# Storing zeros ahead of the result, and last weights in pieces of 5, 2 and 1 eighths, in a decode kernel bound by loads

## The chip, the cores and the metric

The kernel runs on one core of one Trainium2 chip. The metric is the device time of one execution in microseconds (us), as a median of several runs. "The span" is the time from the first to the last instruction in one profiled execution; it is about 1.3 us shorter than the device time. All times inside a profile count from the start of its span.

## The reference, cut to what matters

```python
def reference(A_x, A_k_cache, A_v_cache, A_wq, A_wo, B_x, B_w_in, B_w_sp, B_b_sp, B_w_out, gate_w):
    # A: one token, 32 query heads, 4 key/value heads, 65536 cached positions of 128
    # B: a gated MLP (gelu, layernorm, gate) from 1024 to 3584 and back to 1024
    x = A_x
    g = _sigmoid((x * gate_w).sum(-1, keepdims=True))
    a = _A_ref(x, A_k_cache, A_v_cache, A_wq, A_wo)   # ... attention, then @ wo (4096 x 1024)
    b = _B_ref(x, B_w_in, B_w_sp, B_b_sp, B_w_out)
    return g * a + (1 - g) * b                        # 1 x 1 x 1024, bf16: 2 KB
```

162 MB of caches and weights are read, and 2 KB are written. Nothing but the reading can take long.

## The kernel before: the parts that matter here

The kernel is written with a small recorder. `P(engine, instruction, r=..., w=...)` records one operation with the names that it reads and writes, and semaphore waits are made from these names. All large loads go through the sync queue (SP) in one fixed order, into a ring of SBUF. The last to come are the output weights `wo`, in four parts of 2 MB. The fourth part is cut into pieces, so that PE has little left to do when the last bytes land:

```python
    for i in range(3):
        load([("wo", i, 0)], rows(A_wo, i, 8), VB + 8 * DO * i)
    s3 = kring()
    for c0, c1 in [(0, 4), (4, 6), (6, 8)]:
        load([("wo", 3, c0)], rows(A_wo, 3, 8)[:, DO * c0:DO * c1], s3 + DO * c0)
    # ... everything else of the kernel ...
    for i, c0, c1 in [(0, 0, 8), (1, 0, 8), (2, 0, 8), (3, 0, 4), (3, 4, 6), (3, 6, 8)]:
        sl, keys = use(("wo", i, c0))

        def f(e, i=i, sl=sl, c0=c0, c1=c1):
            for c in range(c0, c1):
                for q in range(4):                    # four column groups of PE, side by side
                    o = DO * (c - c0) + QW * q
                    ins = e.matmul(fb[32 * q:32 * q + 1, 0:QW], ovec[:, 8 * i + c:8 * i + c + 1],
                                   sl[:, o:o + QW], start=False, stop=(i == 3 and c == 7),
                                   tile_position=(0, 32 * q), skip_group_check=True)
            return ins
        P("PE", f, r=[("ovec", i)] + keys, w=["fb"])
        done(("wo", i, c0))
    P("DVE", lambda e: e.tensor_copy(orow[0:97, :], fb[0:97, 0:QW]), w=["orow", "fb"])
    osrc = bass.AP(tensor=arena, offset=OFF["OROW"], ap=[[32 * NA, 4], [1, QW]])
    P("SP", lambda e: e.dma_start(out[0, 0].rearrange("(q n) -> q n", n=QW), osrc), r=["orow"], w=["out"], dma="out")
```

One eighth of a part is 1024 columns: 256 KB, and 4 matmuls on PE. The result lies in 4 rows (partitions 0, 32, 64 and 96) of 256 values, so the store moves 4 rows of 512 bytes.

The waits are emitted in the order of the names, reads first, then writes.

```python
                for d in ws:                          # ... in Recorder.emit
                    if d.dma:
                        handle.wait_ge(dsem[d.dma[0]], d.dma[1])
                    else:
                        handle.wait_ge(sems[d.eng], d.count)
                last = o.fn(handle)
```

## Time and profile before

The median was 383.87 us in 3 runs. These are the lines of the page of the kernel before that say what bounds it: the span in 40 slices (DMA: busy tenths of the 16 DMA engines; GB/s: what they moved), the DMA totals, and the queues with packets, MB and share of the 16 engines' time.

```profile
DMA  9999999999999999999999999999999999999995
GB/s 384 439 435 425 423 417 435 439 436 433 439 425 418 432 430 439 439 432 432 429 420 429 435 439 434 429 435 426 422 432 437 435 432 429 439 425 420 423 425 220
DMA packets 6246, 162.16 MB, mean 424 GB/s; under 512 B 728, under 2 KB 732, under 8 KB 988
...
q1 hardware_dynamic: 6200, 162.01, 98.8%
q8 instruction: 8, 0.13, 0.1%
q14 instruction: 2, 0.02, 0.0%
```

The DMA engines are busy in every slice but the last. The loads set the pace of everything except what follows the last bytes.

The tail is the only place where this change can act. These are the last lines of the chain of waits of the kernel before (start, length, what).

```profile
351.47 28.03 DMA arena<-in_A_wo_dram
379.50 0.04 issue
379.54 0.63 PE fbt L706 x8
380.17 0.02 issue
380.19 0.42 DVE arena L712
```

And this is the line of its timeline for the store behind the cast.

```profile
380.64 0.63 SPq L714 DMA_DIRECT2D out_dram<-arena  x1
```

The last load was issued at 351.47, stood in the queue behind some 25 us of other loads, and landed at 379.50. From there on every step is in series: 8 matmuls, cast, issue of the store, the store's flight. The span ends at 382.33, so the tail behind the landing is 2.83 us.

### The profile page before, as it was taken

What the parts mean: (1) busy time and instruction counts of PE and PEld (TensorE: products, weight loads), DVE (VectorE), ACT (ScalarE), POOL (GpSimd) and SP (SyncE); (2) the same over time, 40 slices, a digit from 0 to 9 for tenths busy, and PEclk for the clock granted to TensorE, in tenths of its full rate; (3) what the DMA queues carried; (4) which work ended last, traced back from release to release, by engine and by line L of the source; (5) the groups of instructions that cost most, each with busy time, mean ns of one, the idle gap of its engine ahead of it and who ended that gap; (6) DMA issues with size and microseconds to landing.
All of it is one profiled execution on the core that took longest, in us unless ns stands there. A gap on an engine that the chain in (4) does not pass through costs nothing.

```text
span 382.3 us, 2522 instructions
## 1 busy us (share of the span) xinstructions
PE 234.6 (61%) x1375; PEld 56.9 (15%) x785; DVE 211.7 (55%) x229; ACT 25.3 (7%) x39; POOL 1.5 (0%) x8
## 2 busy tenths in 40 slices
PE   0055754286687578545793777377938673849344
PEld 0011111111121111101120112012201121112121
DVE  6116952785781698067935980579448914842020
ACT  1000000102030001000210010001200100031000
POOL 1000000000000000000000000000000000000000
PEclk9996998689979599959898998786979988778695
DMA  9999999999999999999999999999999999999995
GB/s 384 439 435 425 423 417 435 439 436 433 439 425 418 432 430 439 439 432 432 429 420 429 435 439 434 429 435 426 422 432 437 435 432 429 439 425 420 423 425 220
DMA packets 6246, 162.16 MB, mean 424 GB/s; under 512 B 728, under 2 KB 732, under 8 KB 988
## 3 DMA queue, kind: packets, MB, share of 16 engines
q1 hardware_dynamic: 6200, 162.01, 98.8%
q8 instruction: 8, 0.13, 0.1%
q14 instruction: 2, 0.02, 0.0%
q10 hardware_dynamic: 36, 0.00, 0.0%
HBM read 162.01 MB, written 0.00 MB: 424 GB/s over the span
## 4 chain that ended last, share of the span: by engine, by line
DMA 61%; PE 19%; DVE 18%; SPq 1%; ACT 1%; issue 1%
DMA arena<-in_A_k_cache_dram 33%; DVE arena L476 13%; DMA arena<-in_B_w_in_dram 8%; DMA arena<-in_A_wo_dram 7%; DMA arena<-in_B_w_out_dram 6%; PE obt L246 6%; DMA arena<-in_A_wq_dram 6%; PE obt L248 5%; PE scp L246 4%; PE scp L248 4%; DVE arena L493 1%; SPq L365 1%; DVE arena L514 1%; DVE arena L464 1%; DVE arena L549 0%
## 5 line engine op out<-in xcount | busy, mean ns | idle before, releaser
L476 DVE STREAM_TRANSPOSE arena<-arena 128x2048 f32<-128x2048 f32 x64 | 145.5, 2295 | 84.5 <-DMA arena<-in_A_k_cache_dram 71.9
L246 PE MATMUL scp<-arena 128*128 128x512 bf16 x256 | 112.5, 439 | 83.4 <-DVE arena L476 61.0
L248 PE MATMUL scp<-arena 128*128 128x512 bf16 x256 | 111.0, 434 | 0.0
L246 PE MATMUL obt<-arena 128*64 128x512 bf16 (+2 forms) x334 | 64.6, 428 | 30.6 <-DMA arena<-in_A_v_cache_dram 12.4
L248 PE MATMUL obt<-arena 128*64 128x512 bf16 (+2 forms) x334 | 64.1, 424 | 0.0
L246 PEld LDWEIGHTS scp<-arena 128*128 128x128 bf16 x256 | 27.5, 107 | 192.2 <-DVE arena L476 93.8
L509 ACT ACTIVATE arena<-arena 128x1024 bf16<-128x1024 f32 x16 | 18.4, 1148 | 237.5 <-DVE arena L505 127.4
L246 PEld LDWEIGHTS obt<-arena 128*64 128x64 bf16 (+1 forms) x334 | 19.4, 116 | 86.6 <-issue 79.1
L493 DVE TENSOR_SCALAR_CACHE_REDUCE arena<-scp 128x1024 f32<-128x1024 f32 x16 | 19.3, 1205 | 9.3 <-PE scp L248 9.3
L514 DVE STREAM_TRANSPOSE arena<-arena 128x1024 bf16<-128x1024 bf16 x16 | 19.4, 1214 | 9.0 <-PE obt L248 6.4
L706 PE MATMUL fbt<-arena 128*1 128x256 bf16 x128 | 6.2, 339 | 5.9 <-DMA arena<-in_A_wo_dram 5.7
L539 DVE RECIPROCAL arena<-mbt 128x1 f32<-128x1 f32 x4 | 0.6, 139 | 14.0 <-PE mbt L535 14.0
L441 DVE CAST arena<-obt 97x1024 bf16<-97x1024 f32 x1 | 1.2, 1224 | 11.5 <-PE obt L248 11.5
L712 DVE CAST arena<-fbt 97x256 bf16<-97x256 f32 x1 | 0.4, 425 | 11.3 <-PE fbt L706 11.3
L588 DVE COPY arena<-obt 128x896 f32<-128x896 f32 x1 | 1.1, 1093 | 9.1 <-PE obt L248 9.1
L464 DVE COPY arena<-arena 32x32 bf16<-32x32 bf16 x16 | 2.7, 166 | 6.2 <-PE scp L248 6.0
L407 PE MATMUL scp<-arena 8*128 8x1 bf16 x8 | 0.6, 197 | 8.4 <-DVE arena L402 8.4
L706 PEld LDWEIGHTS fbt<-arena 128*1 128x1 bf16 x128 | 2.8, 93 | 8.8 <-DMA arena<-in_A_wo_dram 6.7
L595 ACT ACTIVATE arena<-arena 128x28 f32<-128x28 f32 x1 | 0.2, 226 | 52.4 <-DVE arena L594 52.4
L549 DVE SCALAR_TENSOR_TENSOR arena<-obt,arena 128x512 bf16<-128x512 f32 x4 | 3.0, 751 | 0.1
L601 PE MATMUL mbt<-arena 128*128 128x1 f32 x2 | 0.4, 260 | 4.3 <-DVE arena L600 4.3
L509 ACT ACTIVATION_READ_ACCUMULATOR arena<-arena 128x1 f32 x16 | 3.0, 186 | 0.0
(88 smaller groups left out, 47.0 us busy)
## 6 DMA issues: line engine op xcount, KB each, us to landing
arena<-in_A_k_cache_dram SPq DMA_DIRECT2D x16, 4096.0 KB, 38.4
arena<-in_A_v_cache_dram SPq DMA_DIRECT2D x16, 4096.0 KB, 31.1
arena<-in_A_wq_dram SPq DMA_DIRECT2D x2, 4096.0 KB, 16.8
arena<-in_A_wo_dram SPq DMA_DIRECT2D x3, 2048.0 KB, 22.6
arena<-in_B_w_in_dram SPq DMA_DIRECT2D x1, 4096.0 KB, 25.2
arena<-in_B_w_out_dram SPq DMA_DIRECT2D x1, 3584.0 KB, 23.1
arena<-in_B_w_in_dram SPq DMA_DIRECT2D x1, 3072.0 KB, 32.2
arena<-in_A_wo_dram SPq DMA_DIRECT2D x1, 1024.0 KB, 26.5
```

The costliest lines, as they stand in the source:

```text
L246: return e.matmul(*a, **kw)
L248: one = e.matmul(*a, **kw).ins
L365: P("SP", lambda e, o=OFF["RING"] + off + c, m=m, src=src[:, c:c + m]: e.dma_start(arena[:, o:o + m], src), w=[("slot", x) for x in grains ...
L441: P("DVE", lambda e: e.tensor_copy(psb[0:97, :], ob[0:97, :]), w=["psb", "ob"])
L464: P("DVE", lambda e, pb=pb: e.tensor_copy(vw(qpad, 24 + 32 * pb, [[QP, 4], [1, 8]], 32 * pb, 32), vw(qall, 8 * g, [[32, 4], [1, 8]], 32 * ...
L476: P("DVE", lambda e: e.transpose(ktb(i).bitcast(F32), sl[:, 4096 * p:4096 * (p + 1)].bitcast(F32)), r=keys[2 * p:2 * p + 2], w=[("kt", i % ...
L493: P("DVE", lambda e: e.tensor_scalar(scs(n), sc_ps(n), 0.0, None, op0=ALU.add, op1=ALU.max, accum_out=maxc[:, n:n + 1]), w=[("sc", n % NSC ...
L509: P("ACT", lambda e: e.activation(psb, scs(n), ACTF.Exp, bias=gcol(n // NP, K_NB), scale=SCALE, accum_out=lp[:, n:n + 1]), r=[("sc", n % N ...
L514: P("DVE", lambda e: e.transpose(ptsb(n), psb), r=["psb"], w=[("ptsb", n % 2)])
L549: P("DVE", lambda e: e.scalar_tensor_tensor(osc, ob[:, 512:1024], gcol(g, K_FB), osc, op0=ALU.mult, op1=ALU.add), r=[("fh", g, 1), "psb"], ...
L588: P("DVE", lambda e: e.tensor_copy(vw(zr, 0, [[FB4, 2], [32, FC], [1, 32]]), vw(ob, 0, [[512, 2], [1, FC], [FC, 32]])), w=[KZR, "ob"])
L706: ins = e.matmul(fb[32 * q:32 * q + 1, 0:QW], ovec[:, 8 * i + c:8 * i + c + 1], sl[:, o:o + QW], start=False, stop=(i == 3 and c == 7), ti ...
```

## The change

The intent is to shorten that tail in two places. The fourth part of `wo` is cut 5+2+1 instead of 4+2+2, so that only 4 matmuls remain behind the last landing. And the output is stored twice: once with zeros while the last weights are still loading, and once with the result, so that the second store finds whatever is slow at first use already paid for. The smaller bookkeeping grain (`GRAN`) is needed because 5 eighths is no multiple of 2048 columns.

```diff
+    P("POOL", lambda e: e.memset(orow, 0.0), w=["orow"])
...
-    GRAN = 2048
+    GRAN = 1024
...
-    for c0, c1 in [(0, 4), (4, 6), (6, 8)]:
+    for c0, c1 in [(0, 5), (5, 7), (7, 8)]:
         load([("wo", 3, c0)], rows(A_wo, 3, 8)[:, DO * c0:DO * c1], s3 + DO * c0)
+
+    osrc = bass.AP(tensor=arena, offset=OFF["OROW"], ap=[[32 * NA, 4], [1, QW]])
+
+    def store():
+        P("SP", lambda e: e.dma_start(out[0, 0].rearrange("(q n) -> q n", n=QW), osrc), r=["orow"],
+          w=["out"], dma="out")
...
+            if n == len(stream) - 1:
+                store()
...
-          r=keys[2 * p:2 * p + 2], w=[("kt", i % NKT)])
+          r=keys[4 * p:4 * p + 4], w=[("kt", i % NKT)])
...
-    for i, c0, c1 in [..., (3, 0, 4), (3, 4, 6), (3, 6, 8)]:
+    for i, c0, c1 in [..., (3, 0, 5), (3, 5, 7), (3, 7, 8)]:
...
-    osrc = bass.AP(tensor=arena, offset=OFF["OROW"], ap=[[32 * NA, 4], [1, QW]])
-    P("SP", lambda e: e.dma_start(out[0, 0].rearrange("(q n) -> q n", n=QW), osrc), r=["orow"], w=["out"], dma="out")
+    store()
```

## The prediction

> **What bounds the kernel.** The 16 DMA engines: on the page they are busy 9 tenths or more in 39 of 40 slices, at a mean of 424 GB/s for 162 MB. The change touches none of these bytes, so only the tail behind the last weights can move. From the timeline and the trace's single instructions and packets (us from the span's start):
> - The last weights' last packet ends at 379.05, their semaphore lands at 379.50, the first of the last 8 matmuls starts at 379.54.
> - These 8 (256 columns) end at 380.14: two rounds of four column groups, 0.21 us from round to round, at a granted clock of 0.5. The skill's page "TensorE: Matmul & The Clock Gate" gives N / 1.2 GHz for a cold array, 0.213 us: trace and page agree.
> - The cast takes 0.42 us, to 380.62.
> - The output store's issue takes 0.63 us (380.64 to 381.28). Its first packet follows 0.60 us later; the skill's page "DMA: Bandwidth & Descriptors" (latency table) says about 600 ns to the first byte, and the trace agrees. Its last semaphore count comes at 382.29; the span ends at 382.33.
>
> **Pieces of 5, 2, 1 eighths for 4, 2, 2.** The last piece has 4 matmuls, one round, for 8. Its landing should stay near 379.5 (packets of 2 KB for 4 KB: estimate +0.02 us). The first piece lands one eighth later (about 377.64), its 20 matmuls take about 1.24 us, to 378.9; the middle piece lands about there and its 8 matmuls end near 379.5, just when the last piece lands. PE is not late and one round is saved: -0.21 us, all on the critical path.
>
> **The store of zeros.** The sync queue's 43 load issues mostly take 0.33 us (after a wait) or 0.43 (back to back), also where a tensor is read for the first time; the store alone takes 0.63. On the ACT queue the first issue took 0.58 us, the next three 0.27 to 0.29, though they too use few engines. So I take about 0.3 of the 0.63 us for a first use (of this kind of DMA on this queue), which the store of zeros pays at about 351.5, where 25 us of loads are queued and nobody waits. The final issue should fall to 0.33 to 0.43: -0.25 us (estimate). I expect no gain in the 0.60 us to the first packet or the 0.33 us from packet to semaphore.
>
> **Costs.** Four 512-byte packets and their semaphore writes between the last two loads: at most +0.04 us (26 and 9 ns each in the final store). The cast now also waits for the first store's landing, which should come before 379.3, ahead of the cast's start at 379.98. The memset on idle POOL and the finer bookkeeping cost nothing.
>
> **Sum.** -0.21 -0.25 +0.06 = -0.4: last instruction near 381.9. Time 383.45 us, range 382.95 to 383.95 (the runs before spread over 0.4). Faster by over 2%: 0.01; within 2%: 0.98; slower: 0.01.
>
> **What shows each step.** PE's last group has 4 matmuls, about 0.38 us long, starting at the last landing. The final store's issue takes 0.33 to 0.43 us, the first's about 0.6. The cast waits for PE, not for the first store. DMA stays at 424 GB/s.
>
> **What would make it wrong.** The 0.63 us may belong to the kind of store (to DRAM, on four engines), not to a first use: then only -0.15. The zeros may land late behind loads and hold the cast. The first packet of a second write may come earlier: up to -0.3 more. The DMA engines end 1.3 us apart; a drift there may hide it all.

## The result

The changed kernel took 383.59 us (median of 5 runs, 383.43 to 383.75) against 383.75 us before (383.64 to 384.15). The ratio is 0.9993, with a 95% interval of 0.9981 to 1.0005. The interval is 0.9 us wide. The time alone cannot tell whether anything was won; the tails in the traces can, because they repeat to a few thousandths of a us (two traces of each kernel, below). Each tail is read from one profiled execution.

These are the last lines of the chain of waits of the changed kernel.

```profile
350.67 0.62 SPq L349
351.29 0.05 issue
351.34 28.46 DMA arena<-in_A_wo_dram
379.80 0.04 issue
379.84 0.41 PE fbt L715 x4
380.25 0.03 issue
380.28 0.02 DVEq L109
380.30 0.04 issue
380.35 0.42 DVE arena L721
```

And these are the lines of its timeline of the sync queue for the store of zeros, the last load, and the store of the result.

```profile
350.67 0.62 SPq L349 DMA_DIRECT2D out_dram<-arena  x1
351.34 0.39 SPq L374 DMA_DIRECT2D arena<-in_A_wo_dram  x1
380.80 0.54 SPq L349 DMA_DIRECT2D out_dram<-arena  x1
```

Read against the lines of before, four things have moved:

- The last load lands at 379.80, 0.30 us later. This was not forecast.
- PE's last group has 4 matmuls and takes 0.41 us instead of 0.63: -0.22 us.
- Between PE and the cast a line "DVEq L109" has appeared: a wait that stands in an instruction of its own. The cast starts 0.12 us after the last matmul instead of 0.05.
- The final issue takes 0.54 us instead of 0.63.

The profiled span even grew, from 382.33 to 382.42 us. So the questions are: what delayed the landing, what did each half of the change do, and what did the store of zeros warm.

### The profile page after: what moved, and what is told of

Its sections match the earlier page's. It is cut to its first block, busy times and chain, and to the rows that moved or that the text cites. A ratio compares the mean times of both kernels' runs of the same rounds, so it can differ in the third digit from the quotient of the medians.

```text
span 382.4 us, 2525 instructions
## 1 busy us (share of the span) xinstructions
PE 229.7 (60%) x1375; PEld 56.3 (15%) x785; DVE 211.2 (55%) x229; ACT 25.3 (7%) x39; POOL 1.8 (0%) x9
## 4 chain that ended last, share of the span: by engine, by line
DMA 61%; DVE 21%; PE 16%; SPq 1%; issue 1%; ACT 1%; DVEq 0%
DMA arena<-in_A_k_cache_dram 34%; DVE arena L485 15%; DMA arena<-in_B_w_in_dram 8%; DMA arena<-in_A_wo_dram 7%; PE obt L246 6%; DMA arena<-in_B_w_out_dram 6%; PE obt L248 6%; DMA arena<-in_A_wq_dram 6%; PE scp L246 2%; PE scp L248 2%; DVE arena L502 1%; DVE arena L523 1%; SPq L374 1%; DVE arena L558 1%; DVE arena L473 1%
## 5 line engine op out<-in xcount | busy, mean ns | idle before, releaser
L246 PE MATMUL scp<-arena 128*128 128x512 bf16 x256 | 108.7, 425 | 90.7 <-DVE arena L485 65.7
L248 PE MATMUL scp<-arena 128*128 128x512 bf16 x256 | 107.3, 419 | 0.0
L563 PE MATMUL mbt<-arena 128*128 128x128 bf16 x16 | 1.8, 239 | 2.3 <-DVE arena L558 2.3
```

The source lines that it names most:

```text
L246: return e.matmul(*a, **kw)
L248: one = e.matmul(*a, **kw).ins
L563: ins = e.matmul(mb[:, 0:128], sel[:, 128 * c:128 * (c + 1)], osc[:, 128 * c:128 * (c + 1)], start=(c == 0), stop=(c == 3))
```

## The experiments

Eleven kernels ran. The first table gives what the trace shows of each tail; every number is a difference of two times in that trace. "Landing" is the last semaphore count of the last load, "tail" the time from there to the end of the span. "To cast" runs from the end of the last matmul to the start of the cast. "To packet" runs from the end of the final store's issue to its first data packet. "Final issue" is the time that the queue's instruction takes; it is not a separate step ahead of the packet, as "The other queue" shows, so the two columns are best added.

| kernel | landing | tail | last matmuls | to cast | final issue | to packet |
|---|---|---|---|---|---|---|
| before | 379.50 | 2.828 | 0.596 | 0.054 | 0.633 | 0.598 |
| before, again | 379.53 | 2.824 | 0.597 | 0.049 | 0.633 | 0.595 |
| after | 379.80 | 2.622 | 0.383 | 0.120 | 0.535 | 0.636 |
| after, again | 379.59 | 2.619 | 0.383 | 0.121 | 0.536 | 0.639 |
| pieces only | 379.52 | 2.611 | 0.383 | 0.054 | 0.628 | 0.597 |
| zeros only | 379.68 | 2.841 | 0.595 | 0.123 | 0.536 | 0.640 |
| after, waits swapped | 379.47 | 2.552 | 0.383 | 0.051 | 0.535 | 0.639 |
| zeros in two halves | 379.83 | 2.637 | 0.383 | 0.152 | 0.514 | 0.641 |
| pieces, store on ACT | 379.75 | 2.615 | 0.383 | 0.052 | 0.582 | 0.645 |
| pieces, DVE padded | 380.56 | 2.596 | 0.383 | 0.053 | 0.615 | 0.596 |
| pieces, small loads | 379.59 | 2.582 | 0.383 | 0.049 | 0.557 | 0.645 |
| pieces, cast and store on ACT | 379.68 | 2.564 | 0.382 | 0.053 | 0.580 | 0.644 |
| after, cast and stores on ACT | 379.56 | 2.508 | 0.382 | 0.054 | 0.521 | 0.644 |

### Both kernels once more

The edit is none: both kernels ran again unchanged, to learn what repeats.

> The unchanged kernel once more, for a second trace and for the noise of the comparison. Theory (the moment at which the last weights land moves from run to run by a few tenths of a us, because instruction fetches of 16 and 8 KB hold up single DMA engines): the 16 landings of the last load again fall in two groups, 7 early and 9 late by 1.3 to 1.9 us, with one outlier; the last landing lies anywhere from 379.4 to 379.9 us; the store's issue is 0.63 us again. Rival (the landing moved by +0.30 us because of the change): the last landing is 379.50 within 0.05 us. Time ratio 1.000 within 0.001 under both.

Measured: 383.74 us (5 runs) against 383.86 (9 runs of before), ratio 0.9999 (0.9985 to 1.0013). The tail was 2.824 us, the issue 0.633 us, and the landing 379.53. A landing this close to 379.50 fits the rival as well as the theory, so this run does not decide between them; the next one does.

> The changed kernel once more. Theory of varying landings: the last landing is not bound to 379.80, it may fall to 379.5; the rest of the tail repeats: 0.38 us of matmuls, 0.12 us from the last matmul to the cast, 0.53 us for the final store's issue. Rival (change delays the landing): 379.80 within 0.05 us again. Time ratio 0.9990 to 1.0000.

Measured: 383.56 us, ratio 0.9994 (0.9981 to 1.0006). The tail was 2.619 us against 2.622, but the landing moved from 379.80 to 379.59.

What follows: the tail repeats from run to run of a kernel, and the landing does not. The change shortens the tail by 0.206 us (2.828 to 2.622, and 2.824 to 2.619 in the second pair).

### Each half of the change alone

The pieces alone:

```diff
     # the changed kernel, less:
-    P("POOL", lambda e: e.memset(orow, 0.0), w=["orow"])
-            if n == len(stream) - 1:
-                store()
```

> The pieces of 5, 2 and 1 eighths alone, no store of zeros. Both theories: last group of 4 matmuls, 0.38 us; the cast starts 0.05 us after the last matmul (no second wait); the only store's issue takes 0.62 to 0.64 us. From the tail behind the landing this is -0.21 us against before, so ratio 0.9994 within 0.0006 if the landing does not move. If 2 KB packets delay the landing, it lies 0.1 us or more past that of before.

Measured: 383.53 us against 383.86, ratio 0.9993 (0.9980 to 1.0005). The tail is 2.611 us, and the landing, at 379.52, is not delayed by the 2 KB packets. The end of the chain of waits, and the store in the timeline of the sync queue:

```profile
379.56 0.41 PE fbt L712 x4
379.98 0.02 issue
380.00 0.42 DVE arena L718
...
380.45 0.63 SPq L348 DMA_DIRECT2D out_dram<-arena  x1
```

The zeros alone:

```diff
-    for c0, c1 in [(0, 5), (5, 7), (7, 8)]:
+    for c0, c1 in [(0, 4), (4, 6), (6, 8)]:
     # ... and the same pieces in the loop of the matmuls
```

> The store of zeros alone, with pieces of 4, 2 and 2 eighths. Theory: last group of 8 matmuls, 0.60 us; cast 0.12 us after the last matmul, +0.07 for the second wait; final issue 0.53 us, -0.10; sum about -0.03 us, ratio 1.0000 within 0.0006. Rival (zeros delay the landing): the last landing lies at 379.7 or later, and the engine that ends last is one of those that carry a packet of the zeros; ratio 1.0005 or more.

Measured: 383.86 us against 383.86, ratio 1.0000 (0.9988 to 1.0013). The tail is 2.841 us, 0.013 us more than that of before. The landing was 379.68, close to what the rival asked for; the section on the landing shows why it is still not the zeros. The line of the store in the timeline of the sync queue:

```profile
380.90 0.54 SPq L349 DMA_DIRECT2D out_dram<-arena  x1
```

What follows: the pieces give -0.215 us (2.826, the mean of the two traces of before, less 2.611). The zeros give +0.015 us alone and +0.010 on top of the pieces (2.621, the mean of after's two, less 2.611). The store of zeros does act, on three terms that cancel: the final issue is 0.097 us shorter, the first packet comes 0.04 us later after the issue's end (so it comes about 0.06 us earlier after the issue's start), and the cast waits 0.07 us longer.

### The second wait

The cast must now also wait until the store of zeros has read its source. Because "orow" comes first among the names that the cast writes, the wait for the zeros was emitted first and the wait for PE second. In the trace the first emitted wait is carried by the cast, and the second stands in an instruction before it: line "DVEq L109" in the chain above is the wait for PE. So the wait that ends last is the one that must first be taken by a separate instruction. Swapping two names turns this around:

```diff
-    P("DVE", lambda e: e.tensor_copy(orow[0:97, :], fb[0:97, 0:QW]), w=["orow", "fb"])
+    P("DVE", lambda e: e.tensor_copy(orow[0:97, :], fb[0:97, 0:QW]), w=["fb", "orow"])
```

> The changed kernel with the two waits of the last cast in the other order, so that the wait for PE is carried by the cast itself and the long satisfied wait for the zeros stands in the instruction before it. Theory (the second wait costs 0.07 us because the late one stands in an instruction of its own): the cast starts 0.05 to 0.06 us after the last matmul instead of 0.12; the time from the last landing to the end falls from 2.62 to 2.55 us. Rival (any second wait costs it, or the cast is slowed by something else): 0.12 us stays.

Measured: 383.47 us against 383.71, ratio 0.9994 (0.9980 to 1.0007). The chain of waits of this kernel ends so:

```profile
379.47 0.04 issue
379.51 0.41 PE fbt L715 x4
379.92 0.02 issue
379.94 0.42 DVE arena L721
```

The line of the separate wait is gone from the chain, the cast starts 0.051 us after the last matmul, and the tail is 2.552 us, exactly the 0.07 us less that was expected. With this edit the store of zeros is worth 0.059 us (2.611 less 2.552), which agrees with its two other terms: 0.097 less 0.04.

### What the first store warms

The prediction took 0.3 of the 0.63 us of the store's issue for first use. It fell by 0.10. Either that is all, or what was warm had faded again in 30 us of waiting. So the zeros were stored in two halves, back to back:

```diff
             if n == len(stream) - 1:
-                store()
+                for h in range(2):                    # 4 rows of 256 bytes each
+                    P("SP", lambda e, h=h: e.dma_start(out_half(h), orow_half(h)),
+                      r=["orow"], w=[("outz", h)], dma="z%d" % h)
```

(`out_half` and `orow_half` stand here for the two access patterns; the final store waits for both.)

> The zeros in two stores of four rows of 256 bytes, one directly after the other, then the final store 30 us later. Theory of first use, small: the first issue takes 0.62 us, the second and the final one about 0.53, so only 0.10 us is first use and 0.53 belongs to this kind of store. Rival (warmth fades in the 30 us of waiting): the second, back to back, takes 0.30 to 0.43 us and the final one 0.53.

Measured, one look, 383.78 us. Lines of the timeline of the sync queue, in three windows:

```profile
350.53 0.43 SPq L378 DMA_DIRECT2D arena<-in_A_wo_dram  x1
351.00 0.63 SPq L372 DMA_DIRECT2D out_dram<-arena  x1
...
351.68 0.51 SPq L372 DMA_DIRECT2D out_dram<-arena  x1
...
380.86 0.51 SPq L349 DMA_DIRECT2D out_dram<-arena  x1
```

The second issue, directly after the first, takes 0.51 us, and the final one 0.51 us as well. Nothing fades, and no more than 0.12 us of the first issue is first use. The other 0.51 us come with every DMA of this kind. The extra wait shows here too: with a third DMA or engine to wait for, the separate instruction carries two waits, and the cast starts 0.152 us after the last matmul.

Is it stores, or DMAs of four rows? Two loads of four rows of 512 bytes took the zeros' place:

```diff
     # the pieces alone, plus:
             if n == len(stream) - 1:
+                for h in range(2):
+                    P("SP", lambda e, h=h: e.dma_start(
+                        bass.AP(tensor=arena, offset=OFF["PAD"] + 256 * h, ap=[[32 * NA, 4], [1, 256]]),
+                        A_x[0, 0].rearrange("(q n) -> q n", n=256)), w=[("pad", h)], dma="z%d" % h)
     # ... a spare region PAD; the final store waits for both loads
```

> Pieces of 5, 2, 1 without zeros; in their place two loads of four rows of 512 bytes from HBM into spare SBUF, back to back on the sync queue ahead of the last load. If the 0.53 us of a repeated store belongs to DMAs on few engines, the second of these loads takes about 0.5 us; if it belongs to stores, it takes 0.43 us like the loads of 128 rows. And if the first use that costs 0.10 us is that of DMAs on few engines, the first load takes 0.1 us more than the second and the final store then takes 0.53 us; if it is that of a store, the final store takes 0.63 us.

Measured, one look, 383.49 us. The timeline of the sync queue again:

```profile
350.31 0.66 SPq L371 DMA_DIRECT2D arena<-in_A_x_dram  x1
...
351.02 0.51 SPq L371 DMA_DIRECT2D arena<-in_A_x_dram  x1
...
380.52 0.56 SPq L348 DMA_DIRECT2D out_dram<-arena  x1
```

The first load of four rows takes 0.66 us, the second 0.51, and the only store, never issued before, takes 0.56. So on this queue both the 0.51 us and part of the first use come with the DMAs of this shape, whether they load or store. But the store is not warmed as well as by a store of zeros: its issue takes 0.557 us instead of 0.535, its first packet comes 1.202 us after the start of the issue (1.171 to 1.176 behind zeros of four rows of 512 bytes, 1.211 to 1.231 with no earlier DMA of this shape), and the tail is 0.029 us shorter than with the pieces alone, where the zeros with the waits swapped gave 0.059.

What makes "this shape" slow stays open. All DMAs of four rows here, the stores and the two loads, have their rows 32 partitions apart in SBUF (0, 32, 64 and 96). No run has four neighbouring partitions, so the number of rows and their spacing are not told apart.

The Trainium skill, page "DMA: Bandwidth & Descriptors", section "Why a DMA increments its semaphore by 16 and not by 1", says that the number of engines of a DMA (k, at most 16) follows from the size of its slowest dimension, here the rows, and that the issuing sequencer itself then writes the remaining 16 - k increments. The trace agrees for the store: one early semaphore count at 381.66, then four from 382.24 to 382.29. On ACT's queue these writes alone do not make an issue long: in the same trace the last two of its small loads at the start show one early count and one later one, so by the same reading one engine each, and they were issued in 0.27 and 0.29 us. Whether they do on the sync queue, no run shows.

### The other queue

ACT's queue had issued four small loads at the start: 0.58 us the first, 0.27 to 0.29 the rest.

```profile
1.27 0.58 ACTq L271 DMA_DIRECT2D arena<-in_A_x_dram  x1
1.88 0.28 ACTq L271 DMA_DIRECT2D arena<-in_gate_w_dram  x1
2.19 0.27 ACTq L271 DMA_DIRECT2D arena<-in_B_w_sp_dram  x1
2.49 0.29 ACTq L271 DMA_DIRECT2D arena<-in_B_b_sp_dram  x1
```

They write eight neighbouring partitions (the first two) or a single element. If this queue issued the store in 0.3 us, that would be worth more than any store of zeros.

```diff
     # the pieces alone, but:
-        P("SP", lambda e: e.dma_start(out[0, 0].rearrange("(q n) -> q n", n=QW), osrc), r=["orow"],
+        P("ACT", lambda e: e.dma_start(out[0, 0].rearrange("(q n) -> q n", n=QW), osrc), r=["orow"],
```

> Pieces of 5, 2, 1 without zeros, and the only store issued by the ACT queue, whose later small loads took 0.27 to 0.32 us each. If those 0.3 us are what a warm queue needs for a DMA on few engines, the issue takes 0.3 us, and the time from the last landing to the end falls from 2.61 to about 2.3 us. If a store costs more than a load whatever the queue, or the queue is cold again after 370 us, the issue takes 0.5 to 0.65 us and nothing is won.

Measured: 383.51 us against 383.71, ratio 0.9994 (0.9982 to 1.0007). The issue takes 0.582 us and the first packet comes 0.645 us after it, so the tail is 2.615 us: nothing is won over the pieces alone (2.611).

```profile
380.69 0.58 ACTq L348 DMA_DIRECT2D out_dram<-arena  x1
```

From the start of the issue to the first packet it is 1.227 us here and 1.225 us with the pieces alone, although the issue itself is 0.046 us shorter: a shorter issue brings the packet no sooner by itself. What counts for the tail is the time from the issue's start to the packet. The small loads of ACT at the start do not tell what its store costs. They were part of the prediction's evidence for 0.3 us, and it does not carry over. Why those small loads issue in 0.3 us stays open; their rows lie otherwise in SBUF than the store's.

### The landing

In each trace the last load's 16 semaphore counts can be sorted by time. In the kernel before, 7 came within 0.33 us, and the other 9 came 1.55 to 2.05 us after the first. The same sorting for every load shows how this came about. Below are the four latest of the 16, in us behind the first, for the load that lands at 41 us, the one that lands at 282 us (after both q14 packets and five of the eight q8 packets), and the last one (worked out from the semaphore counts, not a view of the profile):

```
                  load at 41 us           load at 282 us          last load
before            0.40 0.40 0.43 0.46     1.88 1.89 1.94 2.10     1.83 1.84 1.88 2.05
before, again     0.23 0.25 0.27 0.30     1.77 1.89 1.89 2.09     1.75 1.87 1.88 2.04
pieces only       0.25 0.29 0.38 0.47     1.66 1.68 1.70 2.16     1.65 1.66 1.75 2.13
after             0.23 0.29 0.29 0.42     1.74 1.81 1.84 2.43     1.72 1.80 1.82 2.44
after, again      0.35 0.35 0.36 0.44     1.69 1.84 1.93 2.24     1.84 1.89 1.94 2.26
zeros only        0.31 0.36 0.39 0.50     1.81 1.81 2.07 2.34     1.80 1.86 2.05 2.34
```

At 41 us all 16 are within half a us. After each 16 KB packet of q8 (8 in the span, 0.9 to 1.1 us each) one more of the 16 is late, 1.4 to 2.1 us behind the first, and it stays late to the end. After each 8 KB packet of q14 (at 57.8 and 260.3 us in the changed kernel, 0.33 us each) one is put back by about 1.0 us, and both times it is the same one (the count at 1.42 us is gone when the one at 2.42 appears). That one is the last of all. In all 13 traces 9 of the 16 are late at the end: eight for eight q8 packets, and this one. The traces do not name the engine of a packet, so which engine is put back is read from the counts alone. Every load has 16 counts, so all engines share in it, and an engine that has been put back does not catch up: the last one's lag changes by at most 0.06 us from the load at 282 us to the last, in these six runs.

This settles the +0.30 us of landing in the changed kernel: its last engine was 2.43 us behind at 282 us, 68 us before the store of zeros was issued, and was still 2.44 behind at the end. In the run of the zeros alone it was 2.34 at 282 us and 2.34 at the end. Over all runs but the padded one the landing is 379.47 to 379.83 with zeros and 379.50 to 379.75 without. The zeros did not add to it, although the last engine did carry one of their four packets (one of their four counts lands at 379.34 in the changed kernel). The lag differs between executions of one kernel (2.44 and 2.26 for the changed one) probably because the engines' starting offsets differ and the engine that is put back twice keeps its own (its offset before the first packet was 0.42 us in the changed kernel).

Whose instructions are they? If q14 brings those of DVE, more DVE instructions must bring one more packet and put the last engine back once more. DVE is idle for 12 us at the start, so 130 instructions cost nothing there:

```diff
     # the pieces alone, plus, after the gate is computed:
+    for i in range(130):
+        P("DVE", lambda e, i=i: e.memset(af("PAD", 1, i)[0:1, :], 0.0), w=[("pad", i)])
     # ... and a spare region PAD
```

> Pieces of 5, 2, 1 without zeros, with 130 memsets of one element on DVE at about 16 us, where DVE waits for 12 us. Theory (the outlier of the last landings is the DMA engine that fetches DVE's instructions, 8 KB each time, and every fetch puts it back by about 1 us for good): the instructions make one more fetch of 8 KB, 3 within the span instead of 2, the outlier lies 3.0 to 3.5 us behind the first landing instead of 2.1 to 2.4, and the time rises by 0.7 to 1.1 us over that of pieces alone, to about 384.5. Rival (the outlier is a slow DMA engine, or has another cause): offsets of 2.1 to 2.4 as before, time 383.5 to 383.7.

Measured: 384.50 us against 383.71, ratio 1.0020 (1.0007 to 1.0033), the only clear difference; against the pieces alone (383.53, in another job) it is +0.97 us, and against the pieces with the store on ACT (383.51, same job, same tail) +0.99 us. The DMA view shows three packets on q14:

```profile
q8 instruction: 8, 0.13, 0.1%
q14 instruction: 3, 0.02, 0.0%
```

The last engine's counts lie 1.36 us behind the first after the first of these packets, 2.37 after the second and 3.30 after the third, each time a step of about 1.0 us. The first of the last load's 16 counts comes at 377.35, as in the other runs (377.30 to 377.53), so it is not the added work on DVE that delays the loads. The chain of waits shows the landing an us later and the same tail behind it:

```profile
350.84 27.88 DMA arena<-in_A_wo_dram
378.72 0.14 issue
378.85 1.71 PE fbt L714 x24
380.57 0.04 issue
380.61 0.41 PE fbt L714 x4
```

What follows: q14 carries DVE's instructions, and the 8 KB more of them cost this kernel about one us at its very end, through the one DMA engine that fetches them. The traces agree: between q14's two packets they count 129 to 133 instructions of DVE in the 12 runs without the padding. That q8 carries PE's instructions is likely (between one of its packets and the next the two traces of before count 237 to 301 instructions of PE, its weight loads and waits included), but no run here tests it.

The Trainium skill, same page, section "Queues, rings and completion order", says that each DMA engine goes round the queues that have work, a packet at a time. That fits one engine's loads being held up by another queue's packet. That section does not say what such a packet costs a kernel.

### A version with a shorter tail than both

If the cast and the store are on one engine, the hop from DVE to the sync queue might be saved, and ACT's copy may be faster than DVE's.

```diff
     # the pieces alone, with the store on ACT, and:
-    P("DVE", lambda e: e.tensor_copy(orow[0:97, :], fb[0:97, 0:QW]), w=["orow", "fb"])
+    P("ACT", lambda e: e.activation(orow[0:97, :], fb[0:97, 0:QW], ACTF.Copy), w=["orow", "fb"])
```

> Pieces of 5, 2, 1 without zeros; the cast of the result and the only store both on ACT. The ACT copy of 97x1024 took 1.02 us where the DVE cast of the same shape took 1.22, so I expect 0.35 us for the 97x256 one instead of 0.42, and no gain in the issue (0.58 us). Time from the last landing to the end 2.5 to 2.6 us against 2.61 for pieces alone; ratio to before 0.9992 within 0.0006.

Measured: 383.56 us against 383.80, ratio 0.9992 (0.9979 to 1.0006). The copy takes 0.384 us instead of 0.425, and the tail is 2.564 us, 0.047 less than the pieces alone. The copy gives 0.040 of this. The hop gives nothing: the store's issue starts 0.030 us after the copy, and 0.028 us after the cast with the pieces alone.

The same with the store of zeros, also on ACT, and the names in the better order:

```diff
     # the changed kernel, with both stores on ACT, and:
-    P("DVE", lambda e: e.tensor_copy(orow[0:97, :], fb[0:97, 0:QW]), w=["orow", "fb"])
+    P("ACT", lambda e: e.activation(orow[0:97, :], fb[0:97, 0:QW], ACTF.Copy), w=["fb", "orow"])
```

> The changed kernel with cast and both stores on ACT and the wait for PE carried by the cast itself. If 0.10 us of an issue is first use, the final issue takes 0.48 us instead of 0.58; no 0.07 us for the second wait. Time from the last landing to the end 2.4 to 2.5 us, ratio to before 0.9989 within 0.0006.

Measured: 383.39 us against 383.80, ratio 0.9990 (0.9978 to 1.0003). Its last timeline lines:

```profile
380.04 0.38 ACT L721 ACTIVATE arena<-fbt 97x256 bf16<-97x256 f32 x1 [31.15 <-PE fbt L715]
380.45 0.52 ACTq L349 DMA_DIRECT2D out_dram<-arena  x1
```

The tail is 2.508 us: 0.32 us shorter than before and 0.11 us shorter than after, and just outside the expected 2.4 to 2.5. The final issue takes 0.521 us, not the expected 0.48: on this queue the store of zeros shortens it by 0.06 us (from 0.580), not by 0.10. It was the lowest median and the shortest tail. Its ratio still includes 1; the claim rests on the tail.

## Why the prediction was right or wrong

The time was right: 383.59 us lies within 382.95 to 383.95, and the change is within 2%. This proves little, because the range was wide enough to hold the kernel before as well (383.75); the tail is the real test, and there 0.4 us was forecast and 0.206 measured. Half of the reasoning was right, and the other half was right in kind but wrong in size.

- "[O]ne round is saved: -0.21 us, all on the critical path." Right. The pieces alone shorten the tail by 0.215 us. The last group of 4 matmuls takes 0.383 us from first start to last end, and PE was never late. The Trainium skill, page "TensorE: Matmul & The Clock Gate", section "Wait — 56ns, not 53.3ns?", gives N / 1.2 GHz for a cold array, an estimate of 0.213 us for 256 columns; the traces show 0.213 (0.596 less 0.383).
- "[P]ackets of 2 KB for 4 KB: estimate +0.02 us" on the landing. Nothing of this kind can be seen: 379.52 with the pieces alone, 379.50 and 379.53 before.
- "The final issue should fall to 0.33 to 0.43: -0.25 us." This is the step that failed. The mechanism exists, but first use is only 0.10 us of the issue (0.633 to 0.535), and the first packet comes 0.04 us later, so 0.06 us remain of 0.25. The other 0.51 to 0.56 us come with a DMA of this shape on this queue. The evidence for 0.3 us came from loads of other shapes: 128 rows on the sync queue, and small loads on ACT, whose store then also took 0.58 us. The prediction had named this possibility.
- "I expect no gain in the 0.60 us to the first packet." There was a loss of 0.04 us. The Trainium skill, page "DMA: Bandwidth & Descriptors", section "Latency and other measured facts", gives about 600 ns to the first byte; the traces show 0.595 to 0.598 us where no DMA of four rows had gone before on the sync queue, and 0.636 to 0.645 us in the other runs.
- "The cast now also waits for the first store's landing [...] The memset on idle POOL and the finer bookkeeping cost nothing." The landing was indeed in time, in every trace. But a second wait is a second instruction, and as emitted it cost 0.07 us. The prediction looked only at when the wait would end, not at what carries it. This one term took back all that the zeros had won.
- "The DMA engines end 1.3 us apart; a drift there may hide it all." Right in kind, and more so than meant: by the counts of the last load the engines end 2.05 us apart in the kernel before, the profiled landing moved by +0.30 us, and the profiled span grew although the tail shrank by 0.21 us. The cause is not the change but instruction fetches that put single DMA engines back, on top of starting offsets that differ from run to run.

The sum that the runs support for the tail is -0.215 (pieces) -0.097 (issue) +0.04 (packet) +0.07 (wait) = -0.20 us, and 0.206 us was measured.

## What to carry to other kernels

When a kernel is bound by loads from end to end, only the series of steps behind the last landing is left to win, and there a few hundredths of a us per step are worth counting: read each step from two traces before believing a median. A new dependency can cost an instruction even when it was satisfied long ago (here 0.07 us), so let the instruction itself carry the wait that ends last and put the old ones ahead of it. And look at which DMA engine lands last and since when: here single engines, put back by instruction fetches far earlier in the run, land 2.0 to 2.4 us after the first at the end, which is more than either half of the change could give.

## What the Trainium skill lacked or had wrong

- "Runtime: NRT & Kernel Launch", section "Instruction fetch mechanics", says that an engine's instructions are fetched in blocks of 16 KiB and calls the cost of a block "mostly hidden". Here DVE's came 8 KB at a time (129 to 133 instructions apart), and 130 more DVE instructions, one more packet, made the kernel about 1.0 us slower. No page says that such a fetch puts a single DMA engine back for the rest of a run of loads: by about 1.0 us for each of the 8 KB packets; after the eight 16 KB packets eight more engines were 1.4 to 2.1 us behind the first.
- "DMA: Bandwidth & Descriptors" gives no issue time by number or place of rows. On the sync queue a DMA of 128 rows mostly issued in 0.33 us after a wait and 0.43 us back to back; one of 4 rows, 32 partitions apart, in 0.51 to 0.56 us, and 0.62 to 0.66 us the first time.
- The same page gives about 600 ns to the first byte; the runs show 0.595 to 0.598 us, or 0.636 to 0.645 us, depending on the queue and on what it had issued before. These are counted from the end of the issue; from its start they are 1.21 to 1.23 us for the first DMA of this shape on its queue and 1.16 to 1.20 us for a later one.
- No page gives the cost of a second semaphore wait on one instruction: 0.07 us when the wait that ends last stands in an instruction of its own, 0.00 when the other one does.
